# Attention scores on four 64x64 tiles of TensorE in place of two 64x128 row tiles, in a linear-attention and mixture-of-experts kernel

## The chip, the core and the metric

One core of a Trainium2 chip runs the whole kernel. The metric is the device time of one execution in microseconds (us). Of the kernel before, three runs stand beside the profile; a fourth, profiled execution is the one whose trace is read here.

## The reference, cut to what matters

Linear attention over 4 batches, 8 heads, 768 positions and head size 64, all in fp32, followed by a top-1 mixture of 8 experts on the 3072 resulting tokens. The change touches the attention alone:

```python
intra = np.einsum('bhic,bhjc->bhij', qb, kb) * Dmask[None]      # scores, decayed and masked
intra = np.einsum('bhij,bhjd->bhid', intra, vb)
inter = np.einsum('bhid,bhde->bhie', qb * lam_pow[None], kv_state)
out[:, :, sl] = intra + inter
kv_state = lam_block[None, :, None, None] * kv_state + np.einsum('bhsd,bhse->bhde', kb_dec, vb)
# then, with x the tokens: expert e of each token, out = gate * (relu(x @ w1[e]) @ w2[e])
```

## The kernel before, in words

The sequence is cut into chunks of 128 positions: 6 to a batch, 24 in all, numbered g = 0 to 23 (g % 6 is the place in its batch). Two chunks are loaded by one DMA of 2 MB (a `load` tile, line 182); three such tiles exist, so the load of a pair of chunks is issued when the chunk pair three before it has been used up. A chunk holds four pairs p of heads; one head of a pair lies on SBUF partitions 0 to 63 and the other on 64 to 127.

The main loop runs over g. In one pass TensorE (PE) makes, in program order:

- the scores of chunk g (line 224): for each pair and each head a product of 64 rows by 128 keys by 128 queries. The two heads of a pair stand on two row tiles of the array, 64 rows by 128 columns each, and write two PSUM tiles `s`, one for each head;
- the part of chunk g-1 that comes from the carried state (line 262, eight products on four 64x64 tiles; left out where chunk g-1 is the first of its batch);
- the output of chunk g-1 from its masked scores (line 273, on 128x64 tiles);
- the state's update from chunk g (line 239, on 128x64 tiles; left out for the last chunk of a batch);
- the transposes of chunk g-2 into tokens with the router's logits beside them (line 285, on the whole array).

VectorE (DVE) makes for each chunk `qd` (line 204, decayed queries) and `kd` (line 209, decayed keys), both from the load; the masked scores `pt`, two products of 128x512 for the two `s` tiles (line 227); the state (lines 243 and 248) and the logits' sum `lg` (line 289). Three times it ranks the tokens of a batch (lines 303 to 354), and once it makes a list of early expert tiles (lines 371 to 475).

`s` has three buffers, and a chunk takes two of them:

```python
sps = [ps.tile([P, NP, P], F32, name="s", bufs=3), ...]
```

so the second `s` tile of chunk g stands in the buffer of the first `s` tile of chunk g-1, and PE's products into it wait until the first `pt` of chunk g-1 has read that one. A wait stands on the first product into the tile; PE and DVE each take their instructions in the order in which they stand, and what is behind a waiting instruction waits too.

The order on each engine is not that of the source: a scheduler sets it when the program is built, from its own estimates of how long instructions take. Line numbers of the changed kernel are one higher from line 224 on.

After the loop come the expert tiles (lines 520 to 666), made of fp32r products on the whole array.

Of the kernel before, what the change touches and what calls it, by code (L numbers as in the profile page):

```python
# [38 lines left out]
def linear_attention_moe(tc, qkv, lam, modality, wg, mbias, w1, w2, out):  # L39
    nc = tc.nc  # L40
    with ExitStack() as ctx:
# [129 lines left out]
        halves2 = [slice(hl * D, (hl + 1) * D) for hl in range(2)]  # L171
# [17 lines left out]
        def loaded(g):  # L189

            t = halves[g // HB][:, :, g % HB]
            kt, qt = (t[:, i].rearrange("p (a t) -> p a t", a=NP) for i in range(2))
            return kt, qt, t[:, 2], t[:, 3]
# [23 lines left out]
        def scores(g):  # L217
            kt, qt, vt, kn = loaded(g)
            pts = []
            sps = [ps.tile([P, NP, P], F32, name="s", bufs=3),  # L220
                   ps.tile([P, NP, P], F32, name="x", bufs=2) if g == 1 else ps.tile([P, NP, P], F32, name="s", bufs=3)]
            for p in range(NP):
                for hl, r in enumerate(halves2):
                    nc.tensor.matmul(sps[hl][:, p, :], kt[r, p, :], qt[r, p, :], start=True, stop=True)  # L224
            for hl in range(2):
                pt = work.tile([P, NP, P], F32, name="pt", bufs=4)
                op = nc.vector.tensor_tensor(out=pt, in0=sps[hl], in1=dk[:, hl], op=ALU.mult)
                pts.append(pt)
            return pts, op
# [500 lines left out]
        for g in range(0, ng + 2):  # L730
# [4 lines left out]
            if g < ng:  # L735
                st1[g], masked = scores(g)
# [55 lines left out]
        hl = [work.tile([P, 2, TT], F32R, name=f"hl{i}", tag=t, bufs=3) for i, t in enumerate(("qd", "qd", "kd", "kd"))]  # L792
# [154 lines left out]
```

## Time and profile before

| | before |
|---|---|
| median of 3 runs | 420.43 us (419.73 to 420.62) |
| the profiled execution | 419.86 us, its span in the trace 418.1 us |
| PE busy in the span | 404.6 us (97%) |
| DVE, ACT, POOL busy | 245.9 us (59%), 188.4 us (45%), 100.0 us (24%) |

The span runs from the first to the last instruction of the trace; the time has 1.8 us more around it. Busy shares are means over the whole program: the attention loop ends at about 116 us, and the expert tiles fill the rest. The trace records every fp32 product as two weight loads and two matmuls, so 8 products are "x16" there. It gives the clock of TensorE that was granted in tenths of full speed (PEclk).

### The profile page before, as it was taken

How to read it: one execution, taken by the hardware profiler on the slowest of the kernel's cores; microseconds unless marked ns; L12 is line 12 of the kernel's file. 1: busy time of each engine (PE TensorE's matmuls, PEld its weight loads, DVE VectorE, ACT ScalarE, POOL GpSimd, SP SyncE). 2: the span in 40 equal slices, each digit the busy share in tenths (PEclk: the TensorE clock that was granted, in tenths of full speed). 3: DMA queues.
4: the chain of work that ended last, by engine and by line, in shares of the span. 5: the costliest groups of instructions: out<-in, count | busy, mean ns of one | idle time of the engine just before them, and what ended most of it. 6: DMA issues, size and time to landing. Idle time of an engine off the chain costs nothing.

```text
span 418.1 us, 9536 instructions
## 1 busy us (share of the span) xinstructions
PE 404.6 (97%) x3665; PEld 356.4 (85%) x3666; DVE 245.9 (59%) x487; ACT 188.4 (45%) x298; POOL 100.0 (24%) x110
## 2 busy tenths in 40 slices
PE   8999999999979999999999999999999999999993
PEld 4687888888879888689898989899998989898982
DVE  4594967788369952168393745638190927456240
ACT  1213343233378151258392736546381927365330
POOL 3110143522540741050322030212121120300001
PEclk9999999999999999999999999999999999999998
DMA  4999989899940039101206567711111020200101
GB/s 145 396 335 381 349 295 330 277 313 318 393 141 3 2 109 401 55 18 45 75 28 184 183 210 250 230 51 52 52 33 69 2 76 27 67 27 2 52 1 48
DMA packets 35093, 63.01 MB, mean 151 GB/s; under 512 B 7381, under 2 KB 21213, under 8 KB 35040
## 3 DMA queue, kind: packets, MB, share of 16 engines
q1 hardware_dynamic: 17056, 43.08, 29.8%
q0 software_dynamic: 4768, 12.69, 9.1%
q10 hardware_dynamic: 13216, 6.56, 5.3%
q8 instruction: 30, 0.49, 0.5%
q14 instruction: 23, 0.19, 0.2%
HBM read 90.97 MB, written 13.68 MB: 250 GB/s over the span
## 4 chain that ended last, share of the span: by engine, by line
issue 44%; PE 22%; DMA 13%; POOL 8%; DVE 6%; POOLq 3%; SPq 3%; ACT 1%; DVEq 0%; ACTq 0%
PE s L224 6%; PE x L285 5%; DMA load<-in_qkv_dram 5%; PE o L273 5%; DMA idx<-inv 4%; POOL out_dram L666 4%; POOL xg L548 3%; DMA xg<-xs,idx 3%; POOLq L844 2%; PE o L262 2%; PE kv L239 2%; DVE w1l L521 1%; SPq L565 1%; DVE w2l L521 1%; PE s L592 1%
## 5 line engine op out<-in xcount | busy, mean ns | idle before, releaser
L588 PE MATMUL s<-xh,w1h 128*128 128x256 f32 x384 | 107.4, 280 | 0.8 <-ACT xh L520 0.8
L592 PE MATMUL s<-xh,w1l 128*128 128x256 f32 x384 | 107.4, 280 | 0.8 <-DVE w1l L521 0.8
L591 PE MATMUL s<-xl,w1h 128*128 128x256 f32 x384 | 107.2, 279 | 0.0
L521 DVE TENSOR_TENSOR w1l<-raw,w1h 128x1024 fp32r<-128x1024 f32 x48 | 58.0, 1218 | 72.6 <-ACT w1h L520 72.6
L588 PE MATMUL o<-w2h,hh 128*128 128x512 f32 x192 | 75.8, 395 | 0.0
L592 PE MATMUL o<-w2h,hl 128*128 128x512 f32 x192 | 74.9, 390 | 0.0
L591 PE MATMUL o<-w2l,hh 128*128 128x512 f32 x192 | 74.8, 390 | 0.0
L588 PEld LDWEIGHTS s<-xh,w1h 128*128 128x128 f32 x384 | 72.2, 188 | 1.6 <-ACT xh L520 1.0
L592 PEld LDWEIGHTS s<-xh,w1l 128*128 128x128 f32 x384 | 72.2, 188 | 1.2 <-DVE w1l L521 1.2
L591 PEld LDWEIGHTS s<-xl,w1h 128*128 128x128 f32 x384 | 72.2, 188 | 0.4
L521 DVE TENSOR_TENSOR w2l<-raw,w2h 128x1024 fp32r<-128x1024 f32 x48 | 58.3, 1217 | 2.0 <-ACT w2h L520 2.0
L520 ACT CAST w1h<-raw 128x1024 fp32r<-128x1024 f32 x48 | 50.0, 1055 | 20.6 <-PE s L591 19.8
L520 ACT CAST w2h<-raw 128x1024 fp32r<-128x1024 f32 x48 | 50.1, 1045 | 0.0
L665 ACT ACTIVATE y<-o,idx 128x512 f32<-128x512 f32 x20 | 13.8, 690 | 75.9 <-PE o L592 45.9
L666 POOL DMA_INDIRECT out_dram<-y,idx x20 | 20.3, 1014 | 114.8 <-ACT y L665 99.4
L607 DVE SCALAR_TENSOR_TENSOR hl<-s,hh 128x512 fp32r<-128x512 f32 x48 | 32.8, 684 | 22.3 <-ACT hh L606 22.3
L592 PEld LDWEIGHTS o<-w2h,hl 128*128 128x128 f32 x192 | 36.0, 188 | 7.6
L591 PEld LDWEIGHTS o<-w2l,hh 128*128 128x128 f32 x192 | 36.1, 188 | 7.2
L588 PEld LDWEIGHTS o<-w2h,hh 128*128 128x128 f32 x192 | 36.1, 188 | 7.1
L548 POOL DMA_INDIRECT xg<-xs,idx x20 | 24.6, 1228 | 72.7 <-PE x L581 68.8
L275 ACT COPY xt<-o 128x256 f32<-128x256 f32 x48 | 17.8, 372 | 49.7 <-PE o L273 45.6
L606 ACT ACTIVATE hh<-s 128x512 fp32r<-128x512 f32 x48 | 28.7, 597 | 19.8 <-PE s L592 19.6
(190 smaller groups left out, 487.4 us busy)
## 6 DMA issues: line engine op xcount, KB each, us to landing
raw<-in_w_dram SPq DMA_DIRECT2D x104, 512.0 KB
load<-in_qkv_dram SPq DMA_DIRECT2D x11, 2048.0 KB
xs<-xn ACTq DMA_DIRECT2D x24, 256.0 KB
load<-in_qkv_dram SPq DMA_DIRECT2D x4, 512.0 KB
spare<-in_w_dram SPq DMA_DIRECT2D x4, 512.0 KB
w1h<-in_w_dram SPq DMA_DIRECT2D x4, 512.0 KB
inv<-pad SPq DMA_DIRECT2D x2, 196.0 KB
inv<-pad SPq DMA_DIRECT2D x2, 192.0 KB
```

The lines of the kernel that those rows point to most:

```text
L224: nc.tensor.matmul(sps[hl][:, p, :], kt[r, p, :], qt[r, p, :], start=True, stop=True)
L273: mm = nc.tensor.matmul(op[half][place(p, hl), i, :], vt[:, (2 * p + hl) * D : (2 * p + hl + 1) * D], pts[hl][:, p, :], start=(c == 0 and ...
L285: nc.tensor.matmul(xp[:, j, : P + E], xt[:, p, :], iw[:, p, :], start=True, stop=True)
L520: cp = nc.scalar.copy(out=hi, in_=src)
L521: df = nc.vector.tensor_tensor(out=lo, in0=src, in1=hi.bitcast(F32), op=ALU.subtract)
L548: last = nc.gpsimd.indirect_dma_start(out=(to or xg)[t][:m], out_offset=None, in_=xs[:rows, :], in_offset=bass.IndirectOffsetOnAxis(ap=idx ...
L588: mm = nc.tensor.matmul(out, ah, bh, start=first, stop=False)
L591: nc.tensor.matmul(out, ah, bl, start=False, stop=False)
L592: return nc.tensor.matmul(out, al, bh, start=False, stop=last)
L606: act = nc.scalar.activation(out=hh[i], in_=hp, func=AF.Relu)
L607: nc.vector.scalar_tensor_tensor(out=hl[i], in0=hp, scalar=0.0, in1=hh[i].bitcast(F32), op0=ALU.max, op1=ALU.subtract)
L666: sc = nc.gpsimd.indirect_dma_start(out=out, out_offset=bass.IndirectOffsetOnAxis(ap=idx[:, t, 0:1], axis=0), in_=y, in_offset=None, bound ...
```

## The change

The weights of one score product, 128 keys, are cut into two halves of 64 keys. Each half goes to its own 64x64 tile of the array and writes its own 64 PSUM partitions. A chunk's scores are then 16 products in place of 8, still of 128 columns (queries) each. What is computed, the two `s` tiles, their readers and all other instructions stay.

```diff
             for p in range(NP):
                 for hl, r in enumerate(halves2):
-                    nc.tensor.matmul(sps[hl][:, p, :], kt[r, p, :], qt[r, p, :], start=True, stop=True)
+                    for s in halves2:
+                        nc.tensor.matmul(sps[hl][s, p, :], kt[r, p, s], qt[r, p, :], start=True, stop=True)
```

In PE's order from the third chunk on, the 16 products stand where the 8 stood. DVE's order changes with it, though no instruction of DVE is added or removed. Three places are shown; in each, `load_...` names the loaded pair of chunks, and the number behind a tile's name only keeps buffers apart.

**First place**, DVE, about the masked scores of chunk 7; the load is that of chunks 8 and 9. Before:

```order
L204 TENSOR_TENSOR qd_603<-load_481,pq_101 128x512
L289 TENSOR_REDUCE lg_360<-xn_592 128x8
L209 TENSOR_TENSOR kd_605<-load_481,dk_86 128x512
L227 TENSOR_TENSOR pt_617<-s_607,dk_86 128x512
L227 TENSOR_TENSOR pt_619<-s_608,dk_86 128x512
L204 TENSOR_TENSOR qd_667<-load_481,pq_101 128x512
L248 TENSOR_TENSOR state2_117<-faded_642,kv_118 128x256
L209 TENSOR_TENSOR kd_669<-load_481,dk_86 128x512
L289 TENSOR_REDUCE lg_360<-xn_645 128x8
```

Of the changed kernel:

```order
L204 TENSOR_TENSOR qd_659<-load_521,pq_101 128x512
L209 TENSOR_TENSOR kd_661<-load_521,dk_86 128x512
L290 TENSOR_REDUCE lg_384<-xn_648 128x8
L204 TENSOR_TENSOR qd_731<-load_521,pq_101 128x512
L209 TENSOR_TENSOR kd_733<-load_521,dk_86 128x512
L228 TENSOR_TENSOR pt_681<-s_663,dk_86 128x512
L228 TENSOR_TENSOR pt_683<-s_664,dk_86 128x512
L249 TENSOR_TENSOR state2_117<-faded_706,kv_118 128x256
L290 TENSOR_REDUCE lg_384<-xn_709 128x8
```

The first `pt` of chunk 7 stood behind one `qd` and one `kd` of the new load, and now stands behind two of each; the `lg` before it stays.

**Second place**, DVE, about the masked scores of chunk 10; the load is that of chunks 12 and 13. Before:

```order
L209 TENSOR_TENSOR kd_881<-load_717,dk_86 128x512
L227 TENSOR_TENSOR pt_831<-s_821,dk_86 128x512
L227 TENSOR_TENSOR pt_833<-s_822,dk_86 128x512
L204 TENSOR_TENSOR qd_930<-load_717,pq_101 128x512
L209 TENSOR_TENSOR kd_932<-load_717,dk_86 128x512
L248 TENSOR_TENSOR state2_117<-faded_864,kv_118 128x256
L289 TENSOR_REDUCE lg_719<-xn_869 128x8
```

Of the changed kernel:

```order
L209 TENSOR_TENSOR kd_969<-load_789,dk_86 128x512
L209 TENSOR_TENSOR kd_1028<-load_789,dk_86 128x512
L228 TENSOR_TENSOR pt_919<-s_901,dk_86 128x512
L228 TENSOR_TENSOR pt_921<-s_902,dk_86 128x512
L204 TENSOR_TENSOR qd_1026<-load_789,pq_101 128x512
L249 TENSOR_TENSOR state2_117<-faded_952,kv_118 128x256
L290 TENSOR_REDUCE lg_791<-xn_957 128x8
```

The `kd` of chunk 13 moved from behind the masked scores of chunk 10 to ahead of them, behind that of chunk 12.

**Third place**, DVE, in the early list, about the masked scores of chunk 16; the load is that of chunks 18 and 19. Before:

```order
L376 TENSOR_REDUCE ntA_1218<-geA_1215 1x8
L404 TENSOR_SCALAR deltaA_1220<-ntA_1218 1x8
L384 TENSOR_TENSOR tmpA_1223<-tri_166,ntA_1218 1x64
L209 TENSOR_TENSOR kd_1317<-load_1107,dk_86 128x512
L385 TENSOR_REDUCE endsA_1222<-tmpA_1223 1x8
L227 TENSOR_TENSOR pt_1266<-s_1256,dk_86 128x512
```

Of the changed kernel:

```order
L377 TENSOR_REDUCE ntA_1346<-geA_1343 1x8
L209 TENSOR_TENSOR kd_1453<-load_1227,dk_86 128x512
L405 TENSOR_SCALAR deltaA_1348<-ntA_1346 1x8
L385 TENSOR_TENSOR tmpA_1351<-tri_166,ntA_1346 1x64
L209 TENSOR_TENSOR kd_1511<-load_1227,dk_86 128x512
L386 TENSOR_REDUCE endsA_1350<-tmpA_1351 1x8
L228 TENSOR_TENSOR pt_1402<-s_1384,dk_86 128x512
```

Two `kd` of the new load stand ahead of the first `pt` of chunk 16 where one stood, and the first of them stands ahead of two small instructions of the list.

## Rows read from the trace of the kernel before

**Rows 1.** The profile's page: the span; busy time, share and number of instructions of PE, its weight loads (PEld), DVE, ACT and POOL; and TensorE's granted clock in 40 equal slices of the span, in tenths.

```profile
span 418.1 us, 9536 instructions
...
PE 404.6 (97%) x3665; PEld 356.4 (85%) x3666; DVE 245.9 (59%) x487; ACT 188.4 (45%) x298; POOL 100.0 (24%) x110
...
PEclk9999999999999999999999999999999999999998
```

**Rows 2.** Four stretches of the span: start and end in us, their length, then busy us (and instructions) of PE, PEld, DVE, ACT and POOL, the granted clock, the DMA engines' mean busy share and GB/s. The first is the loop's beginning, the second the loop from chunk 6 to its end, the third and fourth the expert tiles.

```profile
20.00:37.00 17.00, 15.42 (x236) 13.25 (x237) 12.15 (x27) 4.45 (x12) 1.89 (x2) 1.00 0.99 362
37.00:116.00 79.00, 79.00 (x1260) 69.40 (x1256) 57.65 (x170) 28.73 (x78) 27.82 (x31) 1.00 0.96 327
116.00:150.00 34.00, 31.84 (x226) 28.75 (x225) 29.17 (x100) 20.05 (x29) 13.19 (x12) 1.00 0.17 52
150.00:418.00 268.00, 260.17 (x1792) 233.75 (x1790) 136.85 (x153) 131.04 (x172) 51.55 (x46) 0.99 0.27 90
```

**Rows 3.** What PE's weight loads waited for between 37 and 116 us, the longest group: us in total, times, longest. For PE's matmuls in the same stretch the answer is empty.

```profile
PEld o L273 <- issue: 2.8, 16, 0.2
```

**Rows 4.** The timeline of PE in two passes of the loop (g = 11, then the end of g = 12): start, time from the first record's start to the last record's end, line, tiles, and how many records.

```profile
58.17 1.16 PE L224 MATMUL s<-load 64*128 64x128 f32 x16
59.26 0.67 PE L262 MATMUL o<-qd,state 64*64 64x128 f32 x16
59.86 1.09 PE L273 MATMUL o<-pt,load 128*64 128x128 f32 x16
60.88 1.19 PE L285 MATMUL x<-iw,xt 128*128 128x136 f32 x8
...
63.70 1.09 PE L273 MATMUL o<-pt,load 128*64 128x128 f32 x16
...
64.62 0.64 PE L239 MATMUL kv<-load,kd 128*64 128x64 f32 x16
```

**Rows 5.** The matmul records of three lines: shortest, median and longest duration in ns.

```profile
L224 PE MATMUL s<-load x376: 272/272/373, 6.6 to 110.4; 64*128 64x128 f32 x188
...
L262 PE MATMUL o<-qd,state x320: 269/269/321, 16.6 to 113.8; 64*64 64x128 f32 x160
...
L239 PE MATMUL kv<-load,kd x320: 219/222/270, 13.4 to 108.3; 128*64 128x64 f32 x160
```

**Rows 6.** The chain of waits early in the loop (start, us, what): chunk 3's scores, its pass, and the load of chunks 6 and 7, for which chunk 6's scores wait.

```profile
24.23 1.16 PE s L224 x8
25.39 0.60 PE o L262 x16
...
27.01 0.14 PE kv L239 x5
27.15 9.39 DMA load<-in_qkv_dram
...
36.59 1.16 PE s L224 x16
```

**Rows 7.** The timeline about the first place: DVE, PE's scores of chunk 8 and outputs of chunk 7, and the issue of the load of chunks 12 and 13 on SP.

```profile
42.30 0.69 DVE L204 TENSOR_TENSOR qd<-load,pq 128x512 f32<-128x512 f32 x1 [2.00 <-DMA load<-in_qkv_dram]
...
42.91 0.20 DVE L289 TENSOR_REDUCE lg<-xn 128x8 f32<-128x32 f32 x1
43.03 0.68 DVE L209 TENSOR_TENSOR kd<-load,dk 128x512 f32<-128x512 f32 x1
...
43.63 1.28 DVE L227 TENSOR_TENSOR pt<-s,dk 128x512 f32<-128x512 f32 x2
...
44.59 1.16 PE L224 MATMUL s<-load 64*128 64x128 f32 x16
...
46.28 1.09 PE L273 MATMUL o<-pt,load 128*64 128x128 f32 x16
...
47.42 0.37 SPq L182 DMA_DIRECT2D load<-in_qkv_dram  x1
```

**Rows 8.** The timeline of DVE about the second place (PE's scores of chunk 11 are the first row of rows 4).

```profile
56.74 0.69 DVE L209 TENSOR_TENSOR kd<-load,dk 128x512 f32<-128x512 f32 x1 [2.13 <-DMA load<-in_qkv_dram]
...
57.34 1.28 DVE L227 TENSOR_TENSOR pt<-s,dk 128x512 f32<-128x512 f32 x2
```

**Rows 9.** The timeline about the third place: DVE, then PE's scores of chunk 17.

```profile
80.67 0.23 DVE L404 TENSOR_SCALAR deltaA<-ntA 1x8 f32<-1x8 f32 x1
...
81.51 0.70 DVE L209 TENSOR_TENSOR kd<-load,dk 128x512 f32<-128x512 f32 x1 [0.49 <-DMA load<-in_qkv_dram]
82.13 0.20 DVE L385 TENSOR_REDUCE endsA<-tmpA 1x8 f32<-1x64 f32 x1
82.26 0.67 DVE L227 TENSOR_TENSOR pt<-s,dk 128x512 f32<-128x512 f32 x1
...
84.11 1.16 PE L224 MATMUL s<-load 64*128 64x128 f32 x16
```

**Rows 10.** What the issues of the loads on SP waited for, the longest group: us in total, times, longest.

```profile
SPq L182 <- PE o L273: 52.2, 8, 9.3
```

**Rows 11.** The timeline at the load of chunks 20 and 21: its first reader on DVE, and PE's scores of chunk 19.

```profile
90.88 0.69 DVE L204 TENSOR_TENSOR qd<-load,pq 128x512 f32<-128x512 f32 x1 [0.45 <-DMA load<-in_qkv_dram]
...
92.25 1.16 PE L224 MATMUL s<-load 64*128 64x128 f32 x16
```

## The prediction

> **What bounds the kernel now.** I read the page first, then the stretches, PE's waits, its timeline, and last DVE's timeline where its order changes. PE is busy for 97% of the span [rows 1]. In the stretches the reader is to see two regimes: between 20 and 37 us PE has gaps and the DMA engines are at 0.99, because the chain of waits runs through loads [rows 2, 6]; from 37 to 116 us PE is busy for all 79.00 us and waits for nobody, only 2.8 us of its weight loads' time being "issue" [rows 2, 3]. Behind the loop PE is again busy for 31.84 of 34 us and 260.17 of 268 us [rows 2], on work that starts from the loop's end. So a microsecond taken from PE's work between chunk 6 and chunk 23 is one off the end, unless PE begins to wait. DVE is the one to watch: busy for 57.65 of 79 us [rows 2], and it stands still whenever the next instruction in its order needs a load that has not landed.
>
> **The change on PE.** Score products go from 8 to 16 a chunk, each on a quarter of the array. One pass shows all the prices [rows 4, 5].
>
> - Now, 16 records on two tiles are 8 rounds of two. They last 1.16 us, the first record 0.373 and the usual one 0.272, so a round takes (1.16 - 0.373) / 7 = 0.112 us.
> - Line 262 is the same kind of work on four 64x64 tiles: 16 records, 4 rounds of four, 0.67 us, first record 0.321, usual 0.269. The four of a round start 0.02 us apart in all, so a round takes (0.67 - 0.321 - 0.02) / 3 = 0.11 us, with twice the records of a round of line 224.
> - Sixteen products are 32 records, on four tiles again 8 rounds. The rounds themselves save only 7 times 0.002 to 0.003, 0.02 us: nothing is gained by "four tiles in place of two", since each streams the same 128 columns.
> - The start is shorter: the first record exceeds the usual by 0.10 us with 128 weight columns and by 0.05 with 64. That saves 0.05.
> - Line 262 now follows in the same tiling. Line 273 shows what a change of tiling costs: followed by line 239, in its own tiling, it takes 64.62 - 63.70 = 0.92 us, followed by line 285 60.88 - 59.86 = 1.02. The seam saves 0.10, and line 262's own start 0.05 more.
>
> So a pass saves 0.05 + 0.02 + 0.10 + 0.05 = 0.22 us where line 262 follows the scores, and about 0.06 where it doesn't (chunks 7, 13, 19). Where a rank or a count cuts the scores in two (chunks 9, 15, 16, 21), the second start saves 0.05 more: 0.27.
>
> Ahead of chunk 6, waits for loads hide the rest, but one pass counts: the load of chunks 6 and 7 is issued at 27.15 behind chunk 3's scores, line 262 and line 273 [rows 6]; it goes out 0.21 earlier, and chunk 6 starts 0.21 earlier. From chunk 6: 11 x 0.22 + 4 x 0.27 + 3 x 0.06 = 3.68 us. PE alone gains 3.9.
>
> **The change on DVE.** No instruction is added, but at three places `pt` moves behind work that waits for a load. PE's scores of the next chunk need the buffer that the first `pt` frees.
>
> First place. Chunk 8's scores would start at 44.59 - 0.21 - 0.22 - 0.06 = 44.10 [rows 7]. DVE stood 2.00 us on the load and began `qd` at 42.30; the load follows the one issued 0.21 earlier, so 42.09. Then come `qd` 0.61, `kd` 0.60, `lg` 0.12 (starts in rows 7), now also `qd` and `kd` of the other chunk, 1.20, and the first `pt`, about 0.68 of the pair's 1.28: 45.30, and PE goes on at 45.32. Before, that `pt` ended at 44.31 and PE came at 44.59. PE now stands for **1.2 us**, with line 262, line 273 and the rest of the pass behind it, and ACT's copies and the next load's issue behind those.
>
> Second place. PE would come at 58.17 + 0.73 (the 45.32 against 44.59) - 0.22 - 0.27 - 0.22 = 58.19 [rows 4]. The load's issue waits for line 273 in chunk 8's pass [rows 7, 10], which is 0.51 later than before (0.73 - 0.22). Whether its landing is as late depends on what is still in the queues: between 0 and 0.5. It landed 9.3 us after its issue [rows 7, 8] with the DMA engines nearly full [rows 2], so I take 0.2. Then `kd` 56.94, second `kd` 57.54, first `pt` 58.14 to 58.82: PE stands for **0.65 us** (0.45 to 0.95).
>
> Third place. PE would come at 84.11 + 0.68 (where the second place leaves it) - 0.22 - 0.22 - 0.06 - 0.22 - 0.27 - 0.27 = 83.53 [rows 9]. The load was issued in chunk 14's pass, by then about as before, so it lands at 81.47. First `kd` 0.62, two list instructions 0.36, second `kd` 0.60, a list instruction 0.13, `pt` 0.67: 83.85. PE stands for **0.35 us**.
>
> A fourth place is near the edge: a `qd` that waits for a load at 90.88 moves ahead of chunk 18's `pt`, and chunk 19's scores came at 92.25 [rows 11]. The load goes out about 0.55 earlier (its issue stands in chunk 16's pass): `qd` at 90.35, `pt` done at 91.6, PE at 91.6. I price it at nothing; 0.3 us if the load is that much late.
>
> Elsewhere DVE only changes the order of short instructions that no load holds, and in a loop of 75 us its 57.65 us still leave a quarter free. Ahead of chunk 2 both orders change a little; PE stands there for a load, which hides it. The idle time itself costs no clock: PE had 1.6 us of gaps between 20 and 37 us [rows 2], and the granted clock shows nothing there [rows 1].
>
> **The sum.** 3.9 - 1.2 - 0.65 - 0.35 = 1.7; carried step by step through the passes it is 1.6. The profiled execution took 419.86, so 418.3 for it; the median of the runs is 0.57 above that execution, so **418.8 us**.
>
> **Rivals.**
>
> *DVE is in time.* The loads land early enough, or the buffers of `s` free otherwise than I read. Against it: the 2.00 us wait in rows 7 stands on a load that PE's pace hardly moves. Gain up to 3.9: 416.5 us; with the first stall alone gone about 417.5.
>
> *PE can't be fed that fast.* Scores and line 262 become 24 products in a row, each with half the work of a score product now. The trace shows eight in a row at 0.055 us a product in line 262 and at 0.06 in line 239 ((0.64 - 0.22) / 7, two records a product) [rows 4, 5]; more than eight it never shows, and those may have been queued while slower products ran. Line 224 now runs at 1.09 / 8 = 0.136, which is 0.068 for each of sixteen. Between 0.06 and 0.068 I take 0.064: a round of 0.128, a pass gives back 11 x 0.018 = 0.20 of its 0.22, and the stalls shrink to 1.0, 0.5 and 0.1, because they end at loads. Gain 0.1: **420.3 us**.
> [...]
>
> *The new order alone is left (slower).* If the four tiles give no gain at all, PE comes to chunk 8 at 44.59 - 0, the first `pt` ends at 45.5, and it stands 0.95; then 0.2 at the second place: 1.2 us slower, 421.6 us. It decides as soon as a pass saves less than about 0.06 us. Against it stands line 262.
>
> *Four tiles don't run together*, as two adjacent products share a row tile: 16 rounds of 0.112, 0.9 us more a chunk, 436 us. Line 273 speaks against it, where column tiles sharing all rows keep 16 records within 1.09 us.
>
> **How the numbers follow.** The forecast, 418.0 to 419.6, has 0.56; DVE in time 0.13; not fed fast enough 0.16; the new order alone 0.11; tiles not together 0.04. The range 417.1 to 420.6 takes in the forecast, the third case and the milder half of the second, about 0.8. A run can tell 0.2%, 0.84 us, from no change. Faster than 419.6: 0.56 and 0.13, less a little, 0.67; within 0.2%: 0.18; slower: 0.15.
>
> **What would show it.** In the profile after: line 225 x32 in about 1.1 us from first start to last end, and 0.92 us from its start to line 263's; line 263 then 0.55 instead of 0.60. PE waiting for `pt` at chunks 8, 11 and 17, in that order of size, where it waited for nobody. The loop's last transposes about 1.6 us earlier, and everything behind as long as before. Wrong would be: a pass above 1.6 us for both lines together (PE not fed); no wait for `pt` (my reading of the buffers); a load landing much later than I carry it (then more than 2.2 us of waits).

## The result, and the profile after

The changed kernel takes 422.57 us (median of 9 runs, 421.84 to 425.59) against 419.81 (median of 9, 418.61 to 423.35) for the kernel before beside it: a ratio of 1.006 with a 95% interval of 1.0036 to 1.0084, about 2.8 us slower. The forecast was 418.8, faster, with a range of 417.1 to 420.6.

The page of the changed kernel, the lines that answer to [rows 1], and the row of queue 8, which I take for PE's instruction queue (packets, MB, share of 16 DMA engines):

```profile
span 420.9 us, 10303 instructions
...
PE 404.4 (96%) x4050; PEld 356.5 (85%) x4050; DVE 246.7 (59%) x487; ACT 188.3 (45%) x298; POOL 99.3 (24%) x110
...
PEclk9998999999989999999999999999999999999999
...
q8 instruction: 33, 0.54, 0.5%
```

For the kernel before the last row reads:

```profile
q8 instruction: 30, 0.49, 0.5%
```

PE has 385 matmul records and 384 weight loads more, 769 instructions, and queue 8 brought 3 packets more, while the other instruction queue, 14, has 23 in both. In both traces every packet of queue 8 has 16,384 bytes, so 3 x 16,384 / 769 gives an estimate of 64 bytes an instruction. I come back to that. The clock row, 9s before up to its last slice, has two dips. The stretches that answer to [rows 2], with 37 to 45 us apart:

```profile
20.00:37.00 17.00, 13.95 (x294) 12.04 (x292) 11.64 (x26) 4.45 (x12) 1.90 (x2) 1.00 0.92 330
37.00:45.00 8.00, 7.76 (x144) 7.06 (x146) 5.56 (x11) 1.89 (x5) 0.62 (x1) 0.79 1.00 338
37.00:116.00 79.00, 76.02 (x1514) 67.13 (x1518) 58.30 (x169) 27.35 (x74) 26.66 (x30) 0.98 0.93 309
116.00:150.00 34.00, 32.39 (x234) 29.01 (x235) 27.43 (x97) 19.95 (x30) 13.05 (x12) 0.95 0.29 93
```

Ahead of 37 us PE is busy for 1.5 us less than before, and in the loop, where it had been busy all the time, it now stands for 3 of 79 us. What it waited for between 37 and 116 us, matmuls (before the answer was empty, [rows 3]):

```profile
PE s L225 <- DMA load<-in_qkv_dram: 2.6, 1, 2.6
PE s L225 <- DVE pt L228: 1.8, 2, 1.2
PE o L263 <- issue: 1.0, 1, 1.0
```

PE's timeline in passes 10 to 12 (the pass of rows 4 is the second):

```profile
55.25 1.10 PE L225 MATMUL s<-load 64*64 64x128 f32 x32
57.34 0.67 PE L263 MATMUL o<-qd,state 64*64 64x128 f32 x16 [0.98 <-issue]
...
60.55 0.44 PE L225 MATMUL s<-load 64*64 64x128 f32 x4
61.51 0.98 PE L225 MATMUL s<-load 64*64 64x128 f32 x26 [0.52 <-DVE pt L228]
...
65.11 1.10 PE L225 MATMUL s<-load 64*64 64x128 f32 x32
66.04 0.62 PE L263 MATMUL o<-qd,state 64*64 64x128 f32 x16
66.58 0.66 PE L274 MATMUL o<-pt,load 128*64 128x128 f32 x8
```

The pass at 65.11 is what was forecast: 66.04 - 65.11 = 0.93 us from line 225 to line 263, 66.58 - 66.04 = 0.54 for that. The passes at 55.25 and 60.55 each have a hole. And the chain of waits early in the loop, beside [rows 6]:

```profile
19.89 8.34 DMA xs<-xn
...
28.31 8.88 DMA load<-in_qkv_dram
...
37.24 1.99 PE s L225 x32
39.22 0.85 PE o L263 x16
```

The load of chunks 6 and 7 went out at 28.31 in place of 27.15. SyncE's waits ahead of it read, for xs (the tokens that chunk 0 writes to device memory):

```profile
SPq L182 <- DMA xs<-xn: 1.8, 1, 1.8
```

For the kernel before:

```profile
SPq L182 <- DMA xs<-xn: 0.3, 1, 0.3
```

In the trace chunk 0's write of xs, issued at 19.89, and this load signal their completion on the same semaphore, number 105, and SyncE's wait just ahead of the load, at 28.26, is on 105; the 25 transfers that SyncE and ScalarE issue in the first 44 us use eight semaphores among them. That is why the load waits for the write; the data has no need of it.

The ledger, from the starts of line 225 (line 224 before), pass by pass. From chunk 6's scores to the start of the last transposes it is 36.59 to 114.99 before, 78.40 us, and 37.24 to 117.52 after, 80.28: 1.88 longer. Four passes stick out against the same pass elsewhere: chunk 6 takes 5.58 (4.08 for such a pass; from 37.06 to 40.47 us the trace has the granted clock at 0.50, before and after that at 1.00), chunk 10 5.30 (4.08), chunk 11 4.56 and chunk 17 5.27 (3.62), and chunk 16 has 0.25 too much. That is 1.50 + 1.22 + 0.94 + 1.65 + 0.25 = 5.56 us lost, and so 5.56 - 1.88 = 3.68 us gained in the rest: to the hundredth the 3.68 of the sum. With chunk 6's 0.65 the last transposes start 2.53 later, and the profiled execution is 2.7 longer (422.57 against 419.86): behind the loop little is added, although the clock row's second dip lies there.

The waits for `pt` of chunks 11 and 17 on DVE's side, the second and the third place of the change:

```profile
59.56 1.29 DVE L209 TENSOR_TENSOR kd<-load,dk 128x512 f32<-128x512 f32 x2 [3.48 <-DMA load<-in_qkv_dram]
60.77 1.28 DVE L228 TENSOR_TENSOR pt<-s,dk 128x512 f32<-128x512 f32 x2
...
85.45 1.04 DVE L209 TENSOR_TENSOR kd<-load,dk 128x512 f32<-128x512 f32 x1 [2.54 <-DMA load<-in_qkv_dram]
...
87.36 0.67 DVE L228 TENSOR_TENSOR pt<-s,dk 128x512 f32<-128x512 f32 x1
```

So the gain is there, and three kinds of loss ate it: waits for `pt`, 2.6 us (said: 2.2); the late load, 0.65, with the clock behind it, 1.5; and idle time put down to "issue", 1.5, that I had not thought of. The lower clock alone is not the loss: the execution of the changed kernel with the highest mean clock, 0.998, took 421.84 us, still 2.0 above the median before. The experiments ask whether these are the causes, and whether the four tiles pay without them.

### The profile page after: what moved, and what is told of

It is laid out like the page before. It is cut to its first block, busy times and chain, and to the rows that moved or that the text cites. A ratio compares the mean times of both kernels' runs of the same rounds, so it can differ in the third digit from the quotient of the medians.

```text
span 420.9 us, 10303 instructions
## 1 busy us (share of the span) xinstructions
PE 404.4 (96%) x4050; PEld 356.5 (85%) x4050; DVE 246.7 (59%) x487; ACT 188.3 (45%) x298; POOL 99.3 (24%) x110
## 4 chain that ended last, share of the span: by engine, by line
issue 44%; PE 18%; DMA 16%; DVE 7%; POOL 7%; POOLq 3%; SPq 3%; ACT 0%; DVEq 0%
DMA load<-in_qkv_dram 6%; PE x L286 5%; PE o L274 5%; DMA idx<-inv 5%; PE s L225 4%; POOL out_dram L667 4%; POOL xg L549 3%; DMA xg<-xs,idx 3%; POOLq L845 2%; DMA xs<-xn 2%; DVE w1l L522 2%; PE o L263 2%; PE kv L240 2%; SPq L566 1%; SPq L537 1%
## 5 line engine op out<-in xcount | busy, mean ns | idle before, releaser
L522 DVE TENSOR_TENSOR w2l<-raw,w2h 128x1024 fp32r<-128x1024 f32 x48 | 58.4, 1218 | 2.4 <-ACT w2h L521 2.4
```

Of the source, the lines that this page charges most:

```text
L522: df = nc.vector.tensor_tensor(out=lo, in0=src, in1=hi.bitcast(F32), op=ALU.subtract)
```

## The experiments

### One suspected cause at a time

*a_order.* No `pt` behind a load, by a rule for the scheduler:

```diff
-                st0[g + 1] = prepare(g + 1)
+                st0[g + 1] = prepare(g + 1, masked)   # qd, kd behind pt of the chunk before g
```

> The changed kernel with one rule more for DVE's order: qd and kd of a chunk stand behind the masked scores (pt) of the chunk two before it, so that no pt stands behind a load. Theory 1 (DVE's order makes the stalls): the waits for pt at chunks 11 and 17, 0.96 and 1.67 us long in PE's timeline of the changed kernel, go, and the time falls by 1.8 to 2.4 us, to 420.2 to 420.8. Theory 2 (what is lost ahead of chunk 11, by the late load of chunks 6 and 7, the lower clock behind it and the stall in line 263 at chunk 10, is the larger part): chunk 6 starts at 37.2 as in the changed kernel, and the time stays above that of the kernel before. Rival: the waits move to qd or kd, and the time stays at 422.6.

426.56 us (423.79 to 429.54), ratio 1.0106 (1.0065 to 1.0146): against theory 1's time and the rival's; theory 2's words hold as far as the time is above that before. Waits for `pt` are gone behind chunk 6, yet it is no faster. The profile, of the slowest execution (429.54), shows other losses: chunk 6 at 37.83 after 3.2 us of waiting, the clock at 0.59 between 37 and 45 us, and in chunk 16's pass (PE's timeline)

```profile
84.96 0.42 PE L274 MATMUL o<-pt,load 128*64 128x128 f32 x2 [0.33 <-issue]
86.40 0.46 PE L274 MATMUL o<-pt,load 128*64 128x128 f32 x4 [1.02 <-issue]
87.16 0.27 PE L274 MATMUL o<-pt,load 128*64 128x128 f32 x1 [0.29 <-issue]
87.87 1.31 PE L274 MATMUL o<-pt,load 128*64 128x128 f32 x9 [0.45 <-issue]
```

a line that normally takes 1.09 us crawls for 4.2, one to nine records at a time, and waits for nothing that the profile shows.

*b_late.* The other way round: the kernel before with its eight products, with `qd` or `kd` called ahead of `pt` at chunks 7, 10, 16 and 18 and `pt` put behind them, so that DVE's order is that of the changed kernel there.

> The kernel before, with its 8 score products, and DVE's order of the changed kernel at the four places (chunks 7, 10, 16 and 18). Theory 1: PE waits for pt at chunk 8 (about 0.9 us), chunk 11 and chunk 17, and the kernel is 1.0 to 1.8 us slower than before: 420.8 to 421.6. Rival (the order alone costs nothing, PE comes early only because of the new tiling): within 0.4 us of the kernel before. Chunk 6's scores start at 36.6 under either, since nothing is changed ahead of them.

422.2 us, ratio 1.0028 (1.0004 to 1.0051): the order alone costs about 1.2 us. Its profile puts only 0.2 us of PE's idle time down to `pt`, but by the starts of the scores the pass of chunk 8 takes 4.95 us (4.30 before) and that of chunk 11 4.21 (3.84): 1.0 us at theory 1's first two places. Chunk 16's pass loses another 1.8 (6.58 against 4.82), 0.7 of it "issue" in line 273's place. The time fell where theory 1 put it, for a reason part of which is another.

*e_lane.* The load of chunks 6 and 7 freed of the xs write, by one transfer (that of the small table mb) fewer on SyncE between the two, which is meant to pair it with another transfer's semaphore:

```diff
-            behind(nc.sync.dma_start(out=mb, in_=...), tables)
+            behind(nc.gpsimd.dma_start(out=mb, in_=...), tables)
```

> The changed kernel with the small load of mb issued by GpSimd in place of SyncE. By that the load of chunks 6 and 7 no longer waits for chunk 0's xs write to land, but for the load of chunks 4 and 5, which is needed earlier anyway. Theory 2 (that wait of 1.8 us makes PE stand 2.6 us ahead of chunk 6, and the clock fall to 0.79 between 37 and 45 us): the load is issued by 26.8 in place of 28.31, chunk 6's scores start by 36.2 in place of 37.24, the clock row shows no dip there, and the kernel is 1.5 to 3 us faster than the changed one: 419.6 to 421.1. Rival (the DMA engines are full whenever the load is issued): the load lands within 0.4 us of 37.2, and the time stays at 422.6.

Its mechanism came out: the load goes out at 26.68, chunk 6 starts at 36.20, the clock between 37 and 45 us is 1.00. The gain did not: 425.67 us, ratio 1.0104 (1.0067 to 1.0142). PE now comes to chunk 8 at 44.61, and there is the first place of the forecast:

```profile
44.61 0.43 PE L225 MATMUL s<-load 64*64 64x128 f32 x4
45.69 0.98 PE L225 MATMUL s<-load 64*64 64x128 f32 x26 [0.65 <-DVE pt L228]
```

From chunk 6 on it waits for `pt` at chunks 8, 13 and 19 (2.2 us), and 2 us between 37 and 117 us are "issue". What comes earlier waits longer.

*ae.* Both edits.

> Both edits together in the changed kernel: DVE's order and the small load of mb by GpSimd. If theories 1 and 2 are both right and nothing else is lost, their gains add up: 417.2 to 418.8, 1 to 2.6 us faster than the kernel before. If the stall in line 263 at chunk 10 stays as it is (1.2 us), it lies at the upper end; if it is left and one theory is wrong, 419.5 or more.

424.62 us, ratio 1.0081 (1.0051 to 1.0111). Now PE stands for "issue" (2.6 us up to 112 us) and for DVE's `state`, the very next thing that the rule of a_order left behind a load: 2.9 us. Theories 1 and 2 do not add up to the loss; a third was needed for "issue". The profiled execution is again the slowest of its kernel (428.6).

### What "issue" is

*nl_before, nl_after.* Loads of chunks 6 to 23 left out in both kernels:

```diff
         def load_half(g):
+            if g >= LOADS:
+                return halves[g % LOADS]
```

> The kernel before with the loads of chunks 6 to 23 left out: every later chunk reads one of the first three loaded pairs again, so its results differ and the expert tiles may have other numbers of rows. It is only the partner of nl_after; both have the same data. Expected: PE waits for nobody from chunk 6 on, and the loop from chunk 6's scores to the last outputs lasts 78 to 79 us, as before.

> The changed kernel with the same loads left out. Theory 3 (PE runs out of instructions: four tiles need 176 instructions a chunk in place of 144, they come in pieces of 16 KB by queue 8, and a piece comes late while the loads fill the DMA engines): with the loads gone the pieces come in time, PE has no idle time put down to issue of more than 0.3 us, and the loop from chunk 6 to the last outputs is 3.4 to 3.9 us shorter than that of nl_before. Rival (the sequencer is held up at the border of every piece whatever the DMA engines do, or 16 products in a row can't be kept up): the waits put down to issue are there as in the changed kernel, 1 to 4 us, and the loop gains less than 2.5 us.

nl_before's loop took as long as expected, 35.33 to the last outputs at 113.84 (78.5 us), though it too has a hole of 0.9 us of "issue", at 79.4 us. nl_after's took 77.9, not 3.4 to 3.9 less but 0.6. From chunk 6 to chunk 16 every pass but one is shorter by 0.05, 0.22 or 0.28, as PE's terms say; then line 265 (263 in the others) crawls in chunk 16, as in a_order, with the DMA engines busy for 0.4 of the time:

```profile
78.32 0.30 PE L265 MATMUL o<-qd,state 64*64 64x128 f32 x1 [0.29 <-issue]
79.03 0.45 PE L265 MATMUL o<-qd,state 64*64 64x128 f32 x4 [0.41 <-issue]
80.51 0.52 PE L265 MATMUL o<-qd,state 64*64 64x128 f32 x9 [1.03 <-issue]
```

So full DMA engines are not needed for it: theory 3 in the form put down there falls.

*x_more.* Eight small products more a chunk, on two row tiles.

```diff
+                    if g >= 6:
+                        nc.tensor.matmul(sps[hl][:, p, :8], kt[r, p, :], qt[r, p, :8], start=True, stop=True)
```

> The kernel before, on its two row tiles, with eight small products more (8 columns each) ahead of the score products in each chunk from chunk 6 on, whose results the score products write over. By that PE has the changed kernel's 176 instructions a chunk, but not its tiling; the small products themselves cost about 0.06 to 0.1 us each, 0.5 to 0.8 us a chunk, 9 to 14 us in all. Theory 3: waits put down to issue turn up in PE's rows between 37 and 116 us, at least 0.5 us in all, though less than in the changed kernel, since a chunk lasts longer (4.9 us in place of 4.1); if the longer chunk gives the pieces enough time, none. Rival (the stalls come from 64x64 tiles): none at all.

436.5 us of span, a chunk of the usual kind in 5.3 us, and no idle time for "issue" at all: this tells nothing apart, since theory 3 allowed it.

*l_late.* Four tiles from chunk 18 on alone.

```diff
-                    for s in halves2:
+                    for s in halves2 if g >= 18 else [slice(0, P)]:
```

> Four tiles in chunks 18 to 23 alone; the other chunks have the two row tiles of the kernel before, and DVE's order is that of before. The terms of PE are worth 3 x 0.22 + 0.27 + 2 x 0.06 or so, 1.0 to 1.2 us. Theory 3: 192 instructions more in place of 768, from 88 us on, and the loads end soon after: at most one stall, and the kernel is 0.4 to 1.2 us faster than the kernel before. Rival (PE's gain is never to be had in this kernel): the time is within 0.3 us of the kernel before or above it.

421.45 us, ratio 1.0002 (0.9977 to 1.0028): the median is the rival's, but the interval reaches to 1.0 us faster and so takes in most of theory 3's range. In the profiled execution, the slowest (424.25), 2.0 us of "issue" stand between 105 and 111 us.

*ns_after.* The changed kernel without GpSimd's writes into inv, the table of the tokens' slots.

> The changed kernel without the writes of the slots into inv (GpSimd's indirect transfers of line 360), so the gathers behind the loop find no rows and the time of the expert tiles means nothing; it is read between 37 and 116 us alone. Theory 3a (PE's pieces of instructions come late because the DMA engines are full of loads): the waits put down to issue stay, about 1 us or more. Theory 3b (they come when PE passes into a new piece while GpSimd issues indirect transfers, as at 56.3 us in the changed kernel, where line 360 runs from 56.24 to 57.21): none is left over 0.3 us, chunk 11 starts at most 5.0 us behind chunk 10 (5.3 now), and only the waits for pt at chunks 11 and 17 stay.

No "issue" in PE's matmuls at all between 30 and 120 us, and chunk 11 4.08 us behind chunk 10. For theory 3b, as far as one profile goes.

*s_before, s_after, s_order.* Matmuls that only fill PE's time before the first load are cut into four, so that PE's program is 66 (s_before) or 132 instructions longer ahead of the loop and the same in it:

```diff
+                q = DM // 4
+                for c in [slice(j * q, (j + 1) * q) for j in range(4)] if i < cut else [slice(0, DM)]:
...
```

> The kernel before with 66 instructions more at PE's very start: 11 of the matmuls that only keep PE busy while it waits for the first load are cut into four. Nothing behind them changes but where the borders of the pieces of 256 instructions lie in PE's program: the one that was passed at 81.9 us, 0.3 us behind an indirect transfer, is now passed about 2 us earlier, during one. Theories 3a and 3b: stalls of PE put down to issue turn up where there were none, and the time rises by 0.3 to 2 us. Rival (two row tiles leave PE enough in hand): the time stays within 0.4 us of the kernel before and PE waits for nobody.

> The changed kernel with 132 instructions more at PE's very start, by 22 of the same matmuls cut into four, so that the borders move by half a piece. Theory 3 in either form: the stall in line 263 at chunk 10 (1.2 us) is gone or stands elsewhere, by about half a piece (128 instructions, 3 us), and the time changes by up to 2 us either way. Rival (the stall belongs to that place in the program, whatever the borders): it is there again, at chunk 10, of 1 us or more.

> a_order (the changed kernel, no pt behind a load) with the same 132 instructions more. Theory 3: the 3.9 us of stalls at chunk 16 of a_order stood at a border, which now lies at another chunk; without them the kernel takes 421 to 423 us, against 426.6 of a_order, and if none of the new borders meets a stall, 418.5 to 420. Rival: 426 again.

s_before: 420.21 us, ratio 0.9995 (0.9974 to 1.0017), the rival, with no "issue" and one wait of 0.5 us for `state`. s_after: no "issue" at all, chunk 10 in 4.08 us; 423.09 us, ratio 1.0079 (1.0047 to 1.0110), because PE comes to `pt` at chunks 8, 13 and 17 and waits 2.6 us. s_order: no "issue"; 422.24 us (418.63 to 424.56), ratio 1.0049 (1.0012 to 1.0085), 0.6% below a_order's ratio, with intervals that overlap. What is left in its profile from chunk 7 on is one wait of 2.9 us, DVE's timeline at chunk 18:

```profile
95.41 0.69 DVE L204 TENSOR_TENSOR qd<-load,pq 128x512 f32<-128x512 f32 x1 [5.03 <-DMA load<-in_qkv_dram]
96.02 0.68 DVE L209 TENSOR_TENSOR kd<-load,dk 128x512 f32<-128x512 f32 x1
96.62 0.42 DVE L244 COPY state<-kv 128x256 f32<-128x256 f32 x1
```

The `state` that PE's next kv products need stands behind `qd` and `kd` of a load that lands at 95.4. The rule of a_order was half a rule.

### The three causes taken away, and put back

A better rule: `kd` of a chunk right behind the masked scores of the chunk before it, `qd` (needed a pass later) behind the state's update; neither `pt` nor `state` then stands behind a load for which PE's next scores don't wait anyway.

```diff
-            if 1 <= g < ng - 1:
-                st0[g + 1] = prepare(g + 1)
...
                 st1[g], masked = scores(g)
+            if 1 <= g < ng - 1:
+                next_kd = prepare_k(g + 1, masked)
...
                 passed = carry(g, st0[g][1]) or passed
+            if 1 <= g < ng - 1:
+                st0[g + 1] = prepare_q(g + 1, carried[-1]), next_kd
```

With this rule (order), mb's load on GpSimd (load) and the 132 instructions (shift), each on or off:

> Four tiles, with three edits: DVE's order by rule (kd of a chunk behind pt of the chunk before it, qd behind the state's update, so that neither pt nor the state stands behind a load that PE does not wait for anyway), the small load of mb by GpSimd (as e_lane), and 132 instructions more at PE's start (as s_after). Theory 4 (the four tiles are worth 3.7 us of PE, eaten by waits that these edits take away): no wait for pt or state over 0.3 us and no stall put down to issue between 37 and 116 us, chunk 6 starts by 36.2, and the kernel takes 415.5 to 417.5 us, 2 to 4 us less than the kernel before. Rival (PE can't have these 3.7 us in this kernel, whatever waits go): 419 or more.

> The same three edits on the kernel before, with its two row tiles. Theory 4: the edits give it little, since PE waited for nobody from chunk 6 on: 418.8 to 420.2 us, and fes4 is 3 to 4 us faster than it. Rival: fes4 and fes2 within 1.5 us of each other.

> fes4 with the load of mb back on SyncE, so that the load of chunks 6 and 7 waits for chunk 0's xs write again. Theory 4: chunk 6 starts 1 to 2 us later than in fes4, the clock falls there or not by how long PE is idle, and the kernel is 1 to 3 us slower than fes4. Rival (the late load is made good later, by a loop that waits for loads anyway): within 0.5 us of fes4.

> fes4 without the 132 instructions at the start, so the borders lie as in the changed kernel, where 1.2 us (changed kernel) to 5 us (a_order, ae) went to stalls put down to issue at chunks 10, 16 or 22. Theory 3: such stalls of 1 us or more in all are back, and the kernel is 1 to 4 us slower than fes4. Rival (the stalls came from DVE's order or the late load): none, and the same time as fes4.

> fes4 without the rule for DVE's order: the changed kernel with the load of mb by GpSimd and the 132 instructions at the start. Theory 1, in its first form (the waits for pt at chunks 8, 11 and 17 cost 1.2, 0.65 and 0.35 us, with others where loads come late): PE waits for pt 2 to 4 us in all, and the kernel is 2 to 4 us slower than fes4: 416.8 to 418.8 us. Rival (the order costs nothing once loads are early): within 0.5 us of fes4.

> The changed kernel with the rule for DVE's order alone: the load of chunks 6 and 7 late as there, the program unshifted. Theory 4: no wait for pt, but PE stands idle ahead of chunk 6 for 2 us or more, and stalls put down to issue at the borders of the pieces (chunk 10, chunk 16) are back: 420 to 422.5 us, between 0.3 us above the kernel before and the changed kernel. Rival (the order was the whole loss): 416.5 to 418.5.

| four tiles with | us | ratio to before (95%) |
|---|---|---|
| nothing (the changed kernel) | 422.57 | 1.0060 (1.0036 to 1.0084) |
| load (e_lane) | 425.67 | 1.0104 (1.0067 to 1.0142) |
| shift (s_after) | 423.09 | 1.0079 (1.0047 to 1.0110) |
| load, shift (es4) | 421.34 | 1.0014 (0.9988 to 1.0040) |
| order (f4) | 417.73 | 0.9938 (0.9909 to 0.9967) |
| order, shift (fs4) | 419.74 | 1.0001 (0.9979 to 1.0023) |
| order, load (fe4) | 416.15 | 0.9902 (0.9867 to 0.9937) |
| order, load, shift (fes4) | 414.84 | 0.9878 (0.9846 to 0.9910) |
| two row tiles, all three (fes2) | 418.38 | 0.9958 (0.9938 to 0.9978) |

The medians of the kernel before beside these groups of runs lie between 419.58 and 421.08 us. Kernels of one group (fes4, fes2, fs4, fe4; es4, f4) are compared by their times, others by their ratios; 0.1% is 0.42 us. Four things follow.

**The tiles pay.** fes4 is 5 us faster than the kernel before and 3.5 us faster than fes2, beside the 3.7 forecast for PE (expected: 3 to 4). Both are somewhat faster than their expectations, 415.5 to 417.5 and 418.8 to 420.2. From chunk 6 to chunk 23 fes4 takes 103.96 - 34.35 = 69.61 us and fes2 108.33 - 35.39 = 72.94, 3.33 less, where the terms for these 17 passes give 3.68 - 0.22 = 3.46. PE's waits in fes4 between 37 and 112 us are one line:

```profile
PE x L590 <- ACT xn L295: 0.4, 1, 0.4
```

**DVE's order is the largest cause.** By the ratios, row by row with and without it, the rule is worth 1.2% (alone), 2.0% (with load), 0.8% (with shift) and 1.4% (with both): 5.1, 8.5, 3.3 and 5.7 us, each clear of the intervals. f4 alone beats the kernel before, against my own expectation (420 to 422.5), with the load as late as ever (28.38). Where the price comes from is best seen at chunk 11 of es4, PE and then DVE:

```profile
57.96 0.44 PE L225 MATMUL s<-load 64*64 64x128 f32 x4
60.41 0.78 PE L225 MATMUL s<-load 64*64 64x128 f32 x20 [2.02 <-DVE pt L228]
```

```profile
58.47 1.29 DVE L209 TENSOR_TENSOR kd<-load,dk 128x512 f32<-128x512 f32 x2 [3.62 <-DMA load<-in_qkv_dram]
59.68 1.28 DVE L228 TENSOR_TENSOR pt<-s,dk 128x512 f32<-128x512 f32 x2
```

The load of chunks 12 and 13 lands at 58.4, two `kd` go first, and `pt` frees PE's buffer at 60.3. In f4 DVE has done that `pt` by 56.1 and PE passes the same place without a hole (57.77 to line 271 at 58.70).

Not all that the rule is worth is time waited for `pt`. f4 starts chunk 6 at 37.18, behind 2.75 us of waiting, nearly as the changed kernel does, and comes to chunk 23 in 69.98 us where that took 75.04. Of these 5.1 us, 2.6 are the passes of chunks 11 and 17, 1.5 that of chunk 6, where the clock stayed at 1.00, and 1.2 that of chunk 10, which has no hole (chunk 16 loses 0.25). Whether the rule took these two away as well, or this one execution was without them, no run shows.

**The late load costs up to 4.9 us once the order is mended.** That is the difference between fs4 and fes4 (expected: 1 to 3). Between f4 and fe4 it is 0.4%, which the intervals do not tell from nothing. Without the order rule, taking the late load away was worth 0.65%, 2.7 us, with the shift; without the shift the time rose by 0.4%, which again lies within the intervals. In the profiles chunk 6 starts at 38.75 in fs4 and at 34.35 in fes4, but 2.1 of these 4.4 us are there at chunk 3 already (24.56 against 22.49): in fs4 PE stood for 2.3 us for an early `kd`, and the clock was 0.66 between 15 and 20 us. The load's own part there is about 2.3 us, and 1.6 more in chunk 6's pass (5.70 against 4.08, with the clock at 0.79 between 37 and 45 us). Nor is the shift neutral: with load and shift together (fes4) SyncE waits 3.1 us for another load to land ahead of the load of chunks 6 and 7, which goes out at 20.87; without the shift (fe4) it waits 4.8 us, and the load goes out at 26.36.

The clock between 37 and 45 us was 1.00 in all profiles but one in which PE had stood for 1.4 us or less ahead of chunk 6; the one is x_more, with 0.79 behind 1.15 us. Behind 2.6 to 3.2 us it was 0.59 to 0.79 in four (the changed kernel, a_order, ns_after, fs4) and 1.00 in two (s_after, f4). So the idle time alone does not settle it.

**Much of "issue" stands at the borders of PE's pieces of instructions, but not all.** fe4, unshifted, has four such holes, PE's timeline:

```profile
29.09 0.48 PE L233 MATMUL s<-load 64*64 64x128 f32 x9 [0.66 <-issue]
...
35.55 0.27 PE L282 MATMUL o<-pt,load 128*64 128x128 f32 x1 [0.44 <-issue]
...
56.43 0.67 PE L271 MATMUL o<-qd,state 64*64 64x128 f32 x16 [1.71 <-issue]
...
82.04 0.45 PE L271 MATMUL o<-qd,state 64*64 64x128 f32 x8 [0.48 <-issue]
```

Counted in PE's program (four instructions to an f32 product) they stand at instructions 700, 956, 1724 and 2748: 256, 768 and 1024 apart. At the 64 bytes estimated above, 256 instructions are the 16,384 bytes of one packet of queue 8. The hole of the changed kernel at 57.34 is at 1724 too, that of nl_after at 52.76 within two of it, and those of a_order begin at 2748. Shifted by 132, s_after, s_order, fs4 and fes4 show none up to 112 us; es4 has two of 0.4, at 92.7 and 113.0, and these again stand at such borders, at 3260 and 4028. Unshifted kernels need not have them either: f4 has one of 0.3, ns_after none. And some stand elsewhere. The crawls of e_lane and nl_after in chunk 16 begin about 15 instructions ahead of a border, that of l_late some 75 ahead of one (at 3184), and ae has a hole of 0.45 us at 2922, 82 ahead of one.

Not every crossing costs: PE's matmuls in the kernel before wait for nothing between 37 and 116 us, while one hole at a border of fe4 took 1.71 us. Why some borders cost and others nothing stays open. The hole at 1724 in the changed kernel began while one of GpSimd's writes into inv ran (56.24 to 57.21), and so did the crawls at chunk 16 (a_order, e_lane, ae, nl_after) and l_late's; without these writes (ns_after) there was no hole. But fe4's first two holes have no such write beside them, and fes4 passes borders during writes unharmed. What the holes are worth in time is open as well: fe4 is 1.3 us above fes4 (expected: 1 to 4), which the intervals do not tell from nothing, its profiled execution (418.64) is among its slowest, and fs4 is 0.6% above f4, so the shift as such is no gain.

## Why the prediction was wrong

**PE's terms: right.** A pass 0.22 shorter, 0.27 where a rank cuts it, 0.06 without line 262: 3.68 us in the ledger, 3.5 between fes4 and fes2. What was missed is around them: the profiled execution was forecast at 418.3 and took 422.57, 4.3 more, of which the late load is 0.9, the clock 1.5, "issue" 1.5 and the stalls for `pt` 0.4.

**"It goes out 0.21 earlier, and chunk 6 starts 0.21 earlier": the first step that failed.** I let the issue follow PE's pass of chunk 3 (the scores, line 262 and line 273). But ahead of it SyncE waits for the landing of xs, and by the trace that wait, 0.3 us long, was the one that ended last already in the kernel before: xs landed at 27.08 and the load went out at 27.15. So an earlier PE could not bring the load forward. In the changed kernel xs landed at 28.24, the wait grew to 1.8 us, the load went out 1.16 later and chunk 6 started 0.65 later, 0.86 off the sum. Why xs landed 1.16 later was not tested; its write was issued at 19.89 against 19.94, and queue 8 brought a packet meanwhile, at 24.79.

**"The idle time itself costs no clock": failed.** That was read from 1.6 us of gaps. With 2.6 in one piece ahead of chunk 6 the granted clock was at 0.50 for 3.4 us, and the pass took 1.5 us more. That such a gap does not always cost clock, s_after and f4 show; what decides it stays open.

**The stalls for `pt`: right in kind, place by place off.** First place: none in the changed kernel, because PE itself came at 46.47 in place of 44.10; in e_lane, where it comes at 44.61, 1.08 - 0.16 = 0.9 us are lost there (said 1.2). Second place: 0.94 (0.65); the load landed at 59.6, not 56.9, and PE came at 60.55, not 58.19. Third: 1.65 (0.35); the load landed at 85.4, not 81.5, and PE came at 86.42, not 83.53. Together 2.6 against 2.2 in the profile. But the sum took each load's landing nearly as it was before, and the rule for the order is worth 3.3 to 8.5 us in the runs, more than the stalls. A ring fits that: a late `pt` delays PE, that delays the issue of the next load (line 274 releases it, [rows 10]), and the next `pt` behind it. It was argued and not tested by itself.

**Not in the sum at all: instructions.** 176 a chunk in place of 144, and holes of 1.5 us at two borders, 1724 and 2748. Whether the greater number makes the holes or only the placement is not shown. The rival "PE can't be fed that fast" was right that feeding would matter and wrong as to how: line 225 keeps its 0.93 us for 16 products in every undisturbed pass, 0.058 a product, which is below the 0.064 I took for it. The cost comes in rare lumps, not in each product.

**The slower rival, "the new order alone is left", ended on the right side (421.6) with the wrong mechanism:** it needed tiles without gain; in truth they gained all of their 3.7 and the rest of the kernel lost 6.4. That it came within 1 us is luck.

## What to carry to other kernels

Where one engine is made faster, list every wait of the transfers that it releases, also those now 0.3 us long, and ask which operations that this engine needs stand behind a load in another engine's order: put these first by rule before the edit is judged. Here the same edit cost 2.8 us as it was built, and gained 3.5 where the order, the late load and the shift were the same on both sides. An edit that multiplies instructions is to be judged in several placements of the program, because a stall at a border of the instruction stream may belong to the placement and not to the edit.

## What the runs showed of the hardware

- Queue 8, taken for PE's instructions, has 33 packets of 16,384 bytes in the changed kernel's trace, 1.03 us each in the median (30 in the kernel before); at a border of 256 instructions PE stood for up to 1.71 us (fe4), and in some executions it went on in groups of 1 to 9 records every 0.6 to 1.4 us for 4 us (a_order, begun at a border) or for 3 us (l_late, not begun at one).
- The granted clock's answer to 2.6 to 3.2 us of idle time differs between executions of nearly the same program: 1.00 in two of six, 0.59 in the worst. Behind 1.15 us it fell once (x_more, 0.79).
- Executions of one kernel differ by amounts of their own: fes4 414.0 to 415.8 (6 of them), f4 414.7 to 419.7 (12), a_order 423.8 to 429.5 (6). A single profile may show the slow end.
